# Prologue of a fused attention and MLP block: later first-norm stores, later w2, four tiles transposed on TensorE

## The chip, the cores and the metric

The kernel runs on one core of a Trainium2 chip. The metric is the time on the device in microseconds (us): the median of five runs. A profile of one further execution shows where the time goes.

## The reference

The input x has 2048 rows (tokens) of 1024 values. It is normalised row by row; the result `xn` goes into two branches, and their outputs are added to x. Branch B is what this case is about: it normalises `xn` again, multiplies by w1, applies gelu, shifts four groups of columns by one or two tokens, multiplies by w2, and goes on to a second MLP with w3 and w4. Branch A is an attention with a recurrent memory over segments of 32 tokens; it takes most of the kernel's time and is not touched.

```python
def _layernorm(x, axis=-1, eps=1e-05):
    m = jnp.mean(x, axis=axis, keepdims=True)
    v = jnp.var(x, axis=axis, keepdims=True)
    return (x - m) / jnp.sqrt(v + eps)

def _B_ref(x, w1, w2, w3, w4):
    h = _gelu(_layernorm(x, axis=-1) @ w1)
    ...
    hs = jnp.concatenate([g0, g1, g2, g3], axis=-1) @ w2
    x1 = x + hs
    h2 = _gelu(_layernorm(x1, axis=-1) @ w3) @ w4
    return x1 + h2

x = A_x
xn = _layernorm(x, axis=-1)
return x + _A_ref(xn, A_mem0, A_Wq, A_Wk, A_Wv, A_Wo, A_seg_len) + _B_ref(xn, B_w1, B_w2, B_w3, B_w4)
```

## The kernel before

The 2048 rows are 16 tiles of 128 rows, numbered n = 0 to 15. Work runs in stages on TensorE: phase one (x through both norms, times w1, gelu), phase two (times w2, plus the residual, third norm), phase three (w3 and w4), then the attention. The change lies in phase one and in what its DMAs leave for the start of phase two.

In phase one each tile goes through these steps. `load_x` (L228) brings its rows to the chip. `norm_stats` (L256) takes mean and variance on VectorE (DVE); a power on GpSimd (POOL, L272) makes two factors of them, one for the first norm, one for first and second norm together. So the second norm, `norm2` (L276), works from x directly: on DVE for n below 8 (L281), on ScalarE (ACT) from 8 on (L283). The first norm, `norm1` (L288), makes `xn`, which is kept on the chip as a residual for phase two (`xn_keep`) and stored to memory for the attention (`xn_scratch`, L292).

TensorE needs the second norm's result transposed. For tiles below `NPE` (6) TensorE does that itself: `transposes` (L299), eight matmuls with an identity per tile (L305), copied out by ACT (L306). The other tiles are transposed by a DMA that SyncE (SP) issues (L285) into the tile `xn2T`. `stage1` (L321) then multiplies by w1: for each of eight blocks of output columns, `co`, eight matmuls and one gelu on ACT (L328). It handles one tile (width 128) or a pair (width 256). Tiles 0 to 3 go singly, then the pairs (4,5) to (14,15). Functions handed to `stage1` in `between` are issued after a given block, which is how the preparation of later tiles is placed among ACT's gelus.

In this part every engine's order is the order of the code (a manual schedule); no planner moves work. A DMA issue on SP or ACT uses one of eight completion semaphores in turn, and so waits until the DMA eight issues earlier has landed. SP is a queue in order: what stands behind a waiting issue waits too. The ring of `x` tiles has 10 buffers (so x10 is loaded after the first norm of tile 0 is done with its buffer), that of second-norm tiles 3, and that of `xn2T` 3 pairs.

w2 (2 MB) is loaded by SP ahead of tile 7 in four DMAs (L250); the first two parts of w3 by SP from `norm1` of tiles 12 and 15 (L296), two more in phase two (L433), four at the start of phase three (L442). In phase two (L410) each tile takes 16 matmuls of width 512 (L417), two additions and statistics on DVE, a norm on ACT (L429), a DMA transpose by SP (L430), and a store of 512 KB by POOL (R1, L431); its rings have four buffers.

Of the kernel before, what the change touches and what calls it, by code (L numbers as in the profile page):

```python
# [16 lines left out]
F32 = mybir.dt.float32  # L17
# [6 lines left out]
P = 128  # L24
# [3 lines left out]
NT = S // P  # L28
# [49 lines left out]
def kernel(  # L78
# [16 lines left out]
    nc = tc.nc  # L95
    x_v = A_x[0].rearrange("(n p) d -> p n d", p=P)
# [6 lines left out]
    w2_v = B_w2.rearrange("(k p) n -> p k n", p=P)  # L103
    w3_v = B_w3.rearrange("(k p) n -> p k n", p=P)
# [7 lines left out]
    xn_v = xn_d.rearrange("(n p) d -> p n d", p=P)  # L112
# [78 lines left out]
    with tc.manual_schedule(engines={mybir.EngineType.PE, mybir.EngineType.SP, mybir.EngineType.Pool}), ExitStack() as actx:  # L191
# [6 lines left out]
        with ExitStack() as bctx:  # L198
            w3ctx = bctx.enter_context(ExitStack())
            w3_pool = w3ctx.enter_context(tc.tile_pool(name="w3", bufs=1, side="right"))  # L200
            w3_sb = w3_pool.tile([P, KT, F], BF16)

            w3_at = [0]

            def load_w3():

                c, k0 = divmod(w3_at[0], 4)
                w3_at[0] += 1
                cs = slice(c * (F // 2), (c + 1) * (F // 2))
                nc.sync.dma_start(w3_sb[:, 2 * k0:2 * k0 + 2, cs], w3_v[:, 2 * k0:2 * k0 + 2, cs])  # L210

            with ExitStack() as hctx:
                psum0 = hctx.enter_context(tc.tile_pool(name="psum0", bufs=4, space=PSUM))
# [2 lines left out]
                w2_sb = keep.tile([P, KT, D], BF16)  # L216
                xn_keep = [wpool.tile([P, 4, D], BF16, tag="w", name=f"xnk{i}") for i in range(3)] + [keep.tile([P, 4, D], BF16, name="xnk3")]

                hctx.enter_context(tc.manual_schedule(engines={mybir.EngineType.DVE, mybir.EngineType.Activation}))
                with ExitStack() as p0:  # L220
                    big = p0.enter_context(tc.tile_pool(name="p0big", bufs=1))
                    ring = p0.enter_context(tc.tile_pool(name="p0ring", bufs=3))
                    w1_sb = big.tile([P, KT, D], BF16)
                    NPE = 6

                    xts = {}

                    def load_x(n):  # L228
                        if n < NT:
                            xts[n] = ring.tile([P, D], BF16, tag="xt", bufs=10, name=f"xt{n}")  # L230
                            if n == 0:
                                nc.scalar.dma_start(xts[n][:, 512:], x_v[:, n, 512:])
                                nc.sync.dma_start(xts[n][:, :512], x_v[:, n, :512])
                            else:
                                (nc.gpsimd if n == 12 else nc.sync).dma_start(xts[n][:], x_v[:, n, :])

                    m0 = hTB[:M, 0, 16:16 + D]
                    nc.gpsimd.dma_start(m0, A_mem0[0])
# [7 lines left out]
                        q.dma_start(w1_sb[:, 2 * c:2 * c + 2, :], w1_v[:, 2 * c:2 * c + 2, :])  # L246
                    for n in range(3, 7):
                        load_x(n)
                    for i in range(4):
                        nc.sync.dma_start(w2_sb[:, 2 * i:2 * i + 2, :], w2_v[:, 2 * i:2 * i + 2, :])  # L250
                    for n in range(7, 10):
                        load_x(n)

                    stats = {}

                    def norm_stats(n, part=None):  # L256

                        if n >= NT:
                            return
                        xt = xts[n]  # L260
                        if n not in stats:
                            stats[n] = [ring.tile(shape, F32, tag=tag, bufs=6, name=f"{tag}{n}") for tag, shape in (("st", [P, 2, 6]), ("mv", [P, 2]), ("ab", [P, 2]), ("rr", [P, 2]), ("nm2", [P, 1]))]
                        st, mv, ab, rr, nm2 = stats[n]
                        if part in (None, 0):
                            nc.vector.bn_stats(st[:, 0, :], xt[:, 0:512])
                        if part == 0:
                            return
                        nc.vector.bn_stats(st[:, 1, :], xt[:, 512:1024])
                        nc.vector.bn_aggr(mv[:], st[:])
                        nc.vector.scalar_tensor_tensor(ab[:], epsm[:], mv[:, 1:2], epsa[:], op0=ALU.mult, op1=ALU.add)  # L270
                        for c in (slice(1, 2), slice(0, 1)) if n == 0 else (slice(0, 2),):
                            nc.gpsimd.tensor_tensor(rr[:, c], ab[:, c], neghalf[:, c], op=ALU.pow)  # L272
                        if n >= 8:
                            nc.gpsimd.tensor_scalar(nm2[:], mv[:, 0:1], rr[:, 1:2], -1.0, op0=ALU.mult, op1=ALU.mult)
# [13 lines left out]
                    def norm1(n):  # L288
                        st, mv, ab, rr, nm2 = stats[n]
                        xn = xn_keep[n // 4][:, n % 4]  # L290
                        nc.vector.tensor_scalar(xn, xts[n][:], mv[:, 0:1], rr[:, 0:1], op0=ALU.subtract, op1=ALU.mult)
                        nc.gpsimd.dma_start(xn_v[:, n, :], xn)  # L292
                        if n < 3:
                            load_x(n + 10)
                        if n in (12, 15):
                            load_w3()  # L296
                        return xn

                    def transposes(xn2, xn2T, jj, half, halves=False):  # L299
# [21 lines left out]
                    def stage1(n0, nt, xn2T, between, j0=0):  # L321
                        w = nt * P
                        for co in range(KT):
                            ps = psum.tile([P, 512], F32, tag="mm", bufs=4)
                            for k in range(KT):
                                nc.tensor.matmul(ps[:, :w].rearrange("p (n t) -> p n t", t=P), w1_sb[:, k, co * P:(co + 1) * P],  # L326
                                                 xn2T[:, j0:j0 + nt, k, :], start=(k == 0), stop=(k == KT - 1))
                            nc.scalar.activation(hTB[:, co, 2 + n0 * P:2 + n0 * P + w], ps[:, :w], ACTF.Gelu_apprx_tanh)  # L328
                            for f in between.get(co, ()):
                                f()  # L330
# [13 lines left out]
                    tiles2, xn2s = {}, {}  # L344
# [6 lines left out]
                    def tr(n, half, halves=False):  # L351
                        transposes(xn2s[n], tiles2[n - n % 2], n % 2, half, halves)
# [12 lines left out]
                    nc.gpsimd.memset(hTB[:, :, S + 2:S + 4], 0.0)  # L365
                    load_consts(4)
                    nc.gpsimd.memset(sums[:], 1.0)
                    for n in range(1, 6):
                        if n > 1:
                            norm_stats(n + 1, 0)  # L370
                        norm2_of(n)
                        norm_stats(n + 1, 1 if n > 1 else None)
                        if n > 1:
                            norm1(n - 2)
                        if n == 1:
                            stage1_k(tiles2[0])
                        elif n < 4:
                            stage1(n - 1, 1, tiles2[(n - 1) // 2 * 2], {6 - n: [lambda n=n: tr(n, 0)], 7 - n: [lambda n=n: tr(n, 1)]}, (n - 1) % 2)

                    def ahead(n):  # L380
                        norm_stats(n + 1, 0)
                        norm2_of(n)
                        norm_stats(n + 1, 1)
                        if n == 6:
                            norm1(n - 2)

                    stage1(3, 1, tiles2[2], {0: [lambda: tr(4, 0)], 2: [lambda: tr(4, 1), lambda: ahead(6)], 4: [lambda: tr(5, 0)], 5: [lambda: tr(5, 1), lambda: ahead(7)]}, 1)
                    for n in range(13, NT):
                        load_x(n)

                    def prep(n):
                        norm2_of(n)
                        norm_stats(n + 1)
                        if n == 8:
                            norm1(n - 3)
                        norm1(n - 2)

                    for n0 in range(4, NT, 2):
                        between = {c: [] for c in range(KT)}
                        if n0 + 4 < NT:  # L400
                            between[1 + 2 * (n0 == 4)] += [lambda n0=n0: prep(n0 + 4)]
                            between[4 + 2 * (n0 == 4)] += [lambda n0=n0: prep(n0 + 5)]
                        stage1(n0, 2, tiles2[n0], between)
                    for n in (NT - 2, NT - 1):
                        norm1(n)

                xn3T = [wpool.tile([P, 4, KT, P], BF16, tag="w", name=f"xn3T{tb}") for tb in range(4)]
                with ExitStack() as p2:
                    ring = p2.enter_context(tc.tile_pool(name="p2ring", bufs=4))
                    for n in range(NT):  # L410
                        x1 = ring.tile([P, D], F32, tag="x1")
                        st = ring.tile([P, 2, 6], F32, tag="st")
# [7 lines left out]
                        mv = ring.tile([P, 2], F32, tag="mv")  # L420
# [14 lines left out]
            with ExitStack() as p3:  # L435
# [2 lines left out]
                big = p3.enter_context(tc.tile_pool(name="p3big", bufs=1))  # L438
                ring = p3.enter_context(tc.tile_pool(name="p3ring", bufs=2))
                w4_sb = big.tile([P, FT, D], BF16)  # L440
                for _ in range(4):
                    load_w3()  # L442
                vbT = big.tile([P, H, NSEG], BF16)
                xb = big.tile([P, KT, NSEG], BF16)
                gps = []
# [95 lines left out]
                for tb in range(4):  # L541
# [18 lines left out]
                    for j in range(4):  # L560
                        n = tb * 4 + j
# [214 lines left out]
        ahead = stage_loads([nextB[0]], 0, first_w)  # L776
        for gi_, group in enumerate(groups):
# [3 lines left out]
            for hg in range(8):  # L781
# [8 lines left out]
                if hg < 7:  # L790
                    ahead = stage_loads(Bs, hg + 1, second_w if (gi_, hg) == (0, 0) else ())
                if hg == 7 and gi_ + 1 < len(groups):
                    ahead = stage_loads([nextB[b] for b in groups[gi_ + 1]], 0)
# [236 lines left out]
```

## Time and profile before

| what | us |
|---|---|
| median of five runs (1508.13 to 1509.68) | 1509.32 |
| the profiled execution, its own time | 1508.66 |
| its span, first to last instruction | 1506.5 |
| TensorE (PE) busy in it | 1497.7 |
| phase one ends, the first matmul of phase two starts | 67.03 |
| the first matmul of phase three (w3) starts | about 122.3 |
| first weights of w1 landed, so that stage 1 can start | 8.72 |

All times inside the profile count from the start of the span. A timeline line gives start, duration, engine, line and operation, what is written and read, and how many such instructions were merged; in brackets the engine's idle time before it and what ended it. `SPq`, `ACTq` and `POOLq` are queues that issue DMAs. A line of the chain of waits gives start, duration and what the end of the program hung on in that stretch. Ends of matmuls are modelled, so a busy TensorE may be a little less busy than shown. The share of the DMA engines is above 1 in some short windows, because the packets' recorded times overlap.

DMA traffic by stretch, from the same profile (mean share of the 16 DMA engines, GB/s): 10 to 20 us 1.06 and 378; 20 to 30 us 1.11 and 279; 40 to 50 us 1.17 and 255; 60 to 70 us 0.13 and 51; 100 to 120 us 1.05 and 291.

### The profile page before, as it was taken

Reading aid. Unit: us, or ns where it says so; the run is one execution under the profiler, and the core shown is the slowest. Engines: PE = TensorE matmul, PEld = TensorE weight load, DVE = VectorE, ACT = ScalarE, POOL = GpSimd, SP = SyncE. Lnnn points to the kernel's source line nnn. Section 1 sums busy time; section 2 is a strip of 40 time slices with the busy share of each in tenths; the row PEclk is TensorE's granted clock in tenths of the full one; section 3 lists DMA queues with packets and bytes.
Section 4 is the critical chain, followed back from the end, with each engine's and each line's share of the span. In section 5 each row is a group of like instructions: output and inputs, shape, how many; then the busy total and the mean of one; then the engine's idle time right before and its main releaser. Section 6 shows DMA issues by size and latency. Waiting matters only on the chain.

```text
span 1506.5 us, 24248 instructions
## 1 busy us (share of the span) xinstructions
PE 1497.7 (99%) x9757; PEld 803.5 (53%) x9828; DVE 546.8 (36%) x1148; ACT 502.3 (33%) x1140; POOL 175.9 (12%) x250
## 2 busy tenths in 40 slices
PE   9999999999999999999999999999999999999999
PEld 8744444445454444444466645664665455545555
DVE  8382230100010112211246624651564166516643
ACT  5533103013012011111156614650663166406630
POOL 6231020211211221100000000001000100010001
PEclk9999999999999999999999999999999999999999
DMA  9699752353455777622399957992997299918911
GB/s 306 158 271 322 218 173 93 134 203 113 154 157 143 187 239 252 215 98 84 126 222 248 245 132 175 252 244 69 240 252 203 71 230 223 216 63 207 209 49 51
DMA packets 305426, 272.89 MB, mean 181 GB/s; under 512 B 156022, under 2 KB 272536, under 8 KB 305312
## 3 DMA queue, kind: packets, MB, share of 16 engines
q1 hardware_dynamic: 282656, 188.98, 50.5%
q0 software_dynamic: 21824, 81.08, 15.5%
q8 instruction: 79, 1.29, 0.4%
q10 hardware_dynamic: 832, 1.25, 0.2%
q14 instruction: 35, 0.29, 0.1%
HBM read 190.05 MB, written 45.29 MB: 156 GB/s over the span
## 4 chain that ended last, share of the span: by engine, by line
PE 98%; DMA 1%; issue 0%; ACT 0%; SPq 0%; DVE 0%; ACTq 0%
PE ps L669 30%; PE ps L603 15%; PE pso L727 15%; PE ps L546 13%; PE ps L572 13%; PE ps L417 4%; PE ps L326 3%; PE psO L708 2%; PE psS L684 2%; DMA xn2T<-xn 1%; PE ps L867 1%; PE ps L498 1%; PE gps L481 0%; PE ps L467 0%; DMA w_sb<-in_B_w_dram 0%
## 5 line engine op out<-in xcount | busy, mean ns | idle before, releaser
L669 PE MATMUL ps<-hTb,wt 128*128 128x396 bf16 (+2 forms) x2528 | 484.8, 342 | 0.0
L669 PEld LDWEIGHTS <-wt 128*128 128x128 bf16 x2528 | 236.7, 98 | 175.6 <-DMA wt<-in_A_Wq_dram 0.2
L603 PE MATMUL ps<-wt,xT 128*128 128x512 bf16 x1004 | 220.1, 379 | 1.1
L727 PE MATMUL pso<-wo_sb,oX 128*128 128x512 bf16 (+1 forms) x972 | 208.3, 372 | 1.1
L546 PE MATMUL ps<-xn3T,w_sb 128*128 128x512 bf16 x896 | 196.2, 379 | 0.0
L572 PE MATMUL ps<-w_sb,h3T 128*128 128x512 bf16 x873 | 194.1, 379 | 1.2
L603 PEld LDWEIGHTS <-xT 128*128 128x128 bf16 x1024 | 100.2, 98 | 120.8
L547 ACT ACTIVATE h3T<-ps 128x512 bf16<-128x512 f32 x112 | 66.9, 597 | 290.7 <-PE ps L546 289.8
L727 PEld LDWEIGHTS <-oX 128*128 128x128 bf16 x992 | 96.4, 98 | 107.6
L671 ACT CAST KT<-ps 128x462 bf16<-128x462 f32 (+2 forms) x160 | 81.8, 512 | 202.7 <-PE ps L669 198.5
L572 PEld LDWEIGHTS <-h3T 128*128 128x128 bf16 x896 | 87.0, 98 | 103.6
L546 PEld LDWEIGHTS <-w_sb 128*128 128x128 bf16 x896 | 86.7, 98 | 102.2
L690 DVE TENSOR_REDUCE sums<-sm 99x4 f32<-99x396 f32 (+2 forms) x176 | 97.6, 555 | 114.8 <-ACT sm L688 114.8
L673 ACT ACTIVATE QT<-ps 128x462 bf16<-128x462 f32 (+2 forms) x160 | 84.0, 525 | 120.4 <-PE ps L669 106.2
L605 ACT CAST Vs<-ps 128x512 bf16<-128x512 f32 x64 | 37.5, 586 | 232.1 <-PE ps L603 223.5
L686 DVE TENSOR_TENSOR sm<-psS,c_mask_reg_sb 99x396 f32<-99x396 f32 x152 | 86.7, 571 | 72.4 <-PE psS L684 72.2
L609 DVE CAST Vs<-ps 128x512 bf16<-128x512 f32 x64 | 44.3, 692 | 171.6 <-PE ps L603 166.0
L688 ACT ACTIVATE sm<-sm 99x396 f32<-99x396 f32 (+2 forms) x176 | 93.0, 528 | 34.7 <-DVE sm L686 28.1
L696 DVE TENSOR_TENSOR Pn<-sm,rs 99x396 bf16<-99x396 f32 (+2 forms) x176 | 98.9, 562 | 6.5 <-DMA PT<-Pn 0.6
L734 POOL DMA_DIRECT2D out_dram<-ot x30 | 16.4, 548 | 698.5 <-DVE ot L733 698.5
L573 DVE TENSOR_TENSOR R<-ps,R 128x512 f32<-128x512 f32 x32 | 22.0, 690 | 182.6 <-PE ps L572 172.5
L733 DVE TENSOR_TENSOR ot<-pso,Rt 128x512 bf16<-128x512 f32 (+1 forms) x33 | 22.3, 675 | 166.5 <-PE pso L727 162.3
(131 smaller groups left out, 1049.8 us busy)
## 6 DMA issues: line engine op xcount, KB each, us to landing
wt<-in_A_Wq_dram SPq DMA_DIRECT2D x76, 512.0 KB
wt<-in_A_Wk_dram SPq DMA_DIRECT2D x76, 512.0 KB
wt<-in_A_Wv_dram POOLq DMA_DIRECT2D x24, 1024.0 KB, 6.5
V_scratch<-Vs SPq DMA_DIRECT2D x32, 512.0 KB
V<-V_scratch SPq DMA_DIRECT2D x40, 384.0 KB
R_scratch<-x POOLq DMA_DIRECT2D x16, 512.0 KB, 4.1
R<-R_scratch SPq DMA_DIRECT2D x16, 512.0 KB
R_scratch<-R POOLq DMA_DIRECT2D x16, 512.0 KB, 3.4
```

Source lines behind the costliest of these rows:

```text
L546: nc.tensor.matmul(ps[:].rearrange("p (n t) -> p n t", t=P), w3_sb[:, k, f * P:(f + 1) * P], xn3T[tb][:, :, k, :], start=(k == 0), stop=(k ...
L547: nc.scalar.activation(h3T[:, f, :], ps[:], ACTF.Gelu_apprx_tanh)
L572: nc.tensor.matmul(ps[:], h3T[:, f, j * P:(j + 1) * P], w4_sb[:, f, ch * 512:(ch + 1) * 512], start=(f == 0), stop=(f == FT - 1))
L603: nc.tensor.matmul(ps[:], xT[:, m4 * 4 + j, k, :], wv[:, k, :], start=(k == 0), stop=(k == KT - 1))
L669: nc.tensor.matmul(ps[:, :nb], w[:, k, hh * P:(hh + 1) * P], B["hT"][:, k, :nb], start=(k == 0), stop=(k == KT - 1))
L671: nc.scalar.copy(dst[:, hh, :], ps[:, :nb])
L673: nc.scalar.mul(dst[:, hh, :], ps[:, :nb], scale)
L686: nc.vector.tensor_tensor(sm[:T, :, :T], S3, t["mask"][:].unsqueeze(1).to_broadcast((T, 4, T)), op=ALU.add)
L688: nc.scalar.activation(e[:T, :, :T], sm[:T, :, :T], ACTF.Exp, scale=LN2)
L690: nc.vector.tensor_reduce(ss, e[:T, :, :T], axis=AX.X, op=ALU.add)
L696: nc.vector.tensor_tensor(Pn[:T, :, :T], e[:T, :, :T], rs[:T, :].unsqueeze(2).to_broadcast((T, 4, T)), op=ALU.mult)
L727: nc.tensor.matmul(self.ps[:, :self.w], self.oX[0][:, h, self.oX[1] + self.gl * P:self.oX[1] + (self.gl + 1) * P], wo_sb[:, h, self.cc], s ...
```

## The change

- `NPE` goes from 6 to 4: tiles 4 and 5 are transposed by DMA, as those after them.
- Tiles 4 and 5 go through `stage1` singly, no longer as a pair.
- `norm1` no longer stores its tile and loads no w3. It stands later: for tiles 0 and 1 after the second norms of tiles 4 and 5, for the others two at a time from the preparation of tile 9 on. `load_x(n + 10)` hangs on it for every tile; x10, x11 and x12 are loaded by POOL, the rest by SP.
- The first-norm rows are stored at the end of phase one by SP, in four DMAs of four tiles each.
- w2 is loaded in two halves, after the pairs (6,7) and (12,13); the first two parts of w3 follow the stores, and the last four parts are loaded in two DMAs of double size.
- Preparation of tile n0+3 comes after block 0 of the pair (n0, n0+1), that of n0+4 after block 4; before, those of n0+4 and n0+5 came after blocks 1 and 4. Small statistics tiles get other numbers of buffers.

```diff
-            def load_w3():
+            def load_w3(w=1):
                 c, k0 = divmod(w3_at[0], 4)
-                w3_at[0] += 1
+                w3_at[0] += w
...
-                nc.sync.dma_start(w3_sb[:, 2 * k0:2 * k0 + 2, cs], w3_v[:, 2 * k0:2 * k0 + 2, cs])
+                nc.sync.dma_start(w3_sb[:, 2 * k0:2 * (k0 + w), cs], w3_v[:, 2 * k0:2 * (k0 + w), cs])
...
-                    NPE = 6
+                    NPE = 4
...
-                                (nc.gpsimd if n == 12 else nc.sync).dma_start(xts[n][:], x_v[:, n, :])
+                                (nc.gpsimd if n in (10, 11, 12) else nc.sync).dma_start(xts[n][:], x_v[:, n, :])
...
-                    for i in range(4):
-                        nc.sync.dma_start(w2_sb[:, 2 * i:2 * i + 2, :], w2_v[:, 2 * i:2 * i + 2, :])
                     for n in range(7, 10):
                         load_x(n)
+
+                    def load_w2(i):
+                        nc.sync.dma_start(w2_sb[:, 4 * i:4 * i + 4, :], w2_v[:, 4 * i:4 * i + 4, :])
...
                         nc.vector.tensor_scalar(xn, xts[n][:], mv[:, 0:1], rr[:, 0:1], op0=ALU.subtract, op1=ALU.mult)
-                        nc.gpsimd.dma_start(xn_v[:, n, :], xn)
-                        if n < 3:
-                            load_x(n + 10)
-                        if n in (12, 15):
-                            load_w3()
+                        load_x(n + 10)
...
-                    for n in range(1, 6):
+                    for n in range(1, 4):
...
-                        if n > 1:
-                            norm1(n - 2)
                         if n == 1:
                             stage1_k(tiles2[0])
-                        elif n < 4:
+                        else:
                             stage1(n - 1, 1, tiles2[(n - 1) // 2 * 2], {6 - n: [lambda n=n: tr(n, 0)], 7 - n: [lambda n=n: tr(n, 1)]}, (n - 1) % 2)
-
-                    def ahead(n):
+                    for n in range(4, 8):
                         norm_stats(n + 1, 0)
                         norm2_of(n)
                         norm_stats(n + 1, 1)
-                        if n == 6:
-                            norm1(n - 2)
-
-                    stage1(3, 1, tiles2[2], {0: [lambda: tr(4, 0)], 2: [lambda: tr(4, 1), lambda: ahead(6)], 4: [lambda: tr(5, 0)], 5: [lambda: tr(5, 1), lambda: ahead(7)]}, 1)
-                    for n in range(13, NT):
-                        load_x(n)
+                        if n < 6:
+                            norm1(n - 4)
+                    stage1(3, 1, tiles2[2], {}, 1)
+                    firsts = list(range(2, NT))

                     def prep(n):
                         norm2_of(n)
                         norm_stats(n + 1)
-                        if n == 8:
-                            norm1(n - 3)
-                        norm1(n - 2)
-
-                    for n0 in range(4, NT, 2):
+                        for _ in range(min(2, n - firsts[0]) if n > 8 else 0):
+                            norm1(firsts.pop(0))
+
+                    stage1(4, 1, tiles2[4], {}, 0)
+                    stage1(5, 1, tiles2[4], {4: [lambda: prep(8)]}, 1)
+                    for n0 in range(6, NT, 2):
                         between = {c: [] for c in range(KT)}
-                        if n0 + 4 < NT:
-                            between[1 + 2 * (n0 == 4)] += [lambda n0=n0: prep(n0 + 4)]
-                            between[4 + 2 * (n0 == 4)] += [lambda n0=n0: prep(n0 + 5)]
+                        for n, c in ((n0 + 3, 0), (n0 + 4, 4)):
+                            if n < NT:
+                                between[c] += [lambda n=n: prep(n)]
                         stage1(n0, 2, tiles2[n0], between)
-                    for n in (NT - 2, NT - 1):
-                        norm1(n)
+                        if n0 in (6, 12):
+                            load_w2(n0 // 12)
+                    while firsts:
+                        norm1(firsts.pop(0))
+                    for i in range(4):
+                        nc.sync.dma_start(xn_v[:, 4 * i:4 * i + 4, :], xn_keep[i][:])
+                    for i in range(2):
+                        load_w3()
...
-                for _ in range(4):
-                    load_w3()
+                for _ in range(2):
+                    load_w3(2)
```

More of the change, by code (lines that the diff above doesn't have):

```diff
@@ L261, in norm_stats @@
                         if n not in stats:
-                            stats[n] = [ring.tile(shape, F32, tag=tag, bufs=6, name=f"{tag}{n}") for tag, shape in (("st", [P, 2, 6]), ("mv", [P, 2]), ("ab", [P, 2]), ("rr", [P, 2]), ("nm2", [P, 1]))]
+                            stats[n] = [ring.tile(shape, F32, tag=tag, bufs=10 if tag in ("mv", "rr") else 4, name=f"{tag}{n}") for tag, shape in (("st", [P, 2, 6]), ("mv", [P, 2]), ("ab", [P, 2]), ("rr", [P, 2]), ("nm2", [P, 1]))]
                         st, mv, ab, rr, nm2 = stats[n]
```

## The prediction

> **What bounds the kernel now.** I read the page's busy shares first, then TensorE's timeline over the first 72 us (all that the change touches), then the chain of waits there, then the queue of SyncE, which issues the DMA transposes.
>
> ```profile
> PE 1497.7 (99%) x9757; PEld 803.5 (53%) x9828; DVE 546.8 (36%) x1148; ACT 502.3 (33%) x1140; POOL 175.9 (12%) x250
> ```
>
> TensorE has no idle time to win: 1506.5 - 1497.7 = 8.8 us in the whole span. So the change can give only TensorE work that disappears, or a gap that closes, and it can cost a gap that opens.
>
> ```profile
> 20.39 0.39 PE L305 MATMUL ps<-ident,xn 128*128 128x128 bf16 x4
> ...
> 21.50 0.39 PE L305 MATMUL ps<-ident,xn 128*128 128x128 bf16 x4
> ...
> 22.62 0.39 PE L305 MATMUL ps<-ident,xn 128*128 128x128 bf16 x4
> ...
> 23.29 0.39 PE L305 MATMUL ps<-ident,xn 128*128 128x128 bf16 x4
> 23.52 8.04 PE L326 MATMUL ps<-xn2T,w_sb 128*128 128x128 bf16 x80
> 31.78 7.15 PE L326 MATMUL ps<-xn2T,w_sb 128*128 128x256 bf16 x64 [0.22 <-ACT hTB L328]
> 39.09 28.11 PE L326 MATMUL ps<-xn2T,w_sb 128*128 128x256 bf16 x256 [0.16 <-ACT hTB L328]
> 67.03 5.34 PE L417 MATMUL ps<-w_sb,hTB 128*128 128x512 bf16 x23
> ```
>
> Four groups at L305 are the TensorE transposes of tiles 4 and 5; after the pair (4,5) there are two short gaps, 0.22 and 0.16 us; from 39.09 on the pairs (8,9) to (14,15) run without one, about 7.0 us each (28.11 / 4), and phase two begins at 67.03.
>
> ```profile
> 24.36 5.75 DMA xn2T<-xn
> ...
> 31.48 5.60 DMA xn2T<-xn
> ```
>
> These, from the chain of waits in the same 72 us, are two DMA transposes (tiles 6 and 8) with the time from issue to landing: 5.6 to 5.8 us, with x loads, w2 and first-norm stores in flight. A transpose with little beside it is faster; from the timelines of SyncE and VectorE at 190 us:
>
> ```profile
> 190.40 1.23 SPq L450 DMA_TRANSPOSE xr<-xn_scratch  x1
> ```
>
> ```profile
> 193.68 1.22 DVE L452 TENSOR_REDUCE xb<-xr 128x32 bf16<-128x1024 bf16 x1 [0.81 <-DMA xr<-xn_scratch]
> ```
>
> The reader waited for it until 193.68: 3.3 us from issue. And one directly behind a large load is slower; SyncE's timeline, then its waits:
>
> ```profile
> 50.84 0.57 SPq L210 DMA_DIRECT2D w_sb<-in_B_w_dram  x1
> 52.17 1.23 SPq L285 DMA_TRANSPOSE xn2T<-xn  x1
> 53.45 0.58 SPq L210 DMA_DIRECT2D w_sb<-in_B_w_dram  x1
> ```
>
> ```profile
> SPq L430 <- DMA xn2T<-xn: 5.5, 1, 5.5
> ```
>
> Tile 15's transpose was issued at 52.17, behind 896 KB of w3; SyncE, free at 54.03, waited 5.5 us more for it, to 59.5: 7.3 us from issue. Nobody needed it before 60 us. These three latencies, 3.3, 5.7 and 7.3, decide this case.
>
> [...] The trace shows the slow state only at the start (12 warm-up matmuls in 5.30 us, 442 ns each, where 128x512 later takes 10.74 / 49 = 219 ns)[...].
>
> **The change, part by part.** The order of the changed program and what each instruction waits for are read from its instructions; times from the rows above.
>
> Tiles 4 and 5 off TensorE: 2 x 8 matmuls of 128x128 go. The chain gives 0.22 us to four, so 4 x 0.22 = 0.89 us less. Their four ACT evictions (0.59 us each, L306) go too, beside TensorE: nothing.
>
> Tiles 4 and 5 single: 128 matmuls of width 128, at 0.0558 us (0.446 per output block of eight), for 64 of width 256 at 0.109 us (0.873 per block): 7.14 against 6.98, +0.16 us.
>
> Gaps: the ACT norm of tile 8 stood waiting for tile 6's transpose until 30.11 and held the gelus back; it now waits for an old TensorE tile. Both gaps, 0.38 us, can go.
>
> First norms late: norm1 of tiles 0 and 1 (0.54 us each on VectorE) moves behind the second norms of tiles 4 and 5; the others follow from tile 9 on. It shortens VectorE's chain less than it seems, as norm2 then waits for POOL's power (0.7 to 0.9 us, L272). The chain per tile is norm2 0.46, half statistics 0.72, aggregation and scaling 0.4, then POOL's answer about 0.9 later, 2.5 us; with a norm1 behind the scaling 2.7. From norm2 of tile 2 at 12.93 (its row before, unmoved) I get norm2 of tiles 4, 5, 6, 7 at 17.9, 20.6, 23.3, 25.8, against 18.3, 21.0, 23.75, 26.5 in VectorE's rows. Norm2 of 6 and 7 gain a wait for the transposes of 4 and 5 (buffer reuse); their statistics and stores queue behind it on VectorE. With the first-norm stores and w2 out of the way, the load of the first 4.5 MB at the 380 GB/s of these windows ends near 14 us, so these transposes run nearly alone: 3.3 us, or 4.4, which is what tile 7 took before beside three x loads and a store (27.03 to 31.45 in the record of semaphores).
> - Tile 4: issued 18.5, landed 21.8 to 22.9; TensorE wants it at 24.41 - 0.89 = 23.5. No gap.
> - Tile 5: 21.2 to 24.5-25.6, wanted at 27.1. Tile 7: 26.4 to 29.7-30.8, wanted at 23.5 + 7.14 = 30.66. At most 0.1.
>
> Second norms of tiles 9, 11, 13, 15 now come after the first output block of the pair just before theirs. From there to the need are 7.0 - 0.87 = 6.1 us; gelu (0.4) and norm (1.24) take 1.6 of it: each of these transposes has about 4.5 us. Before, they were issued a pair earlier. Alone (3.3) or in light traffic (4.4) they make it: tile 9 (block 0 of the pair (6,7) ends at 31.5, so issued 33.2 and landed by 37.6, wanted at 37.65), 13 and 15.
>
> Tile 11 doesn't. SyncE's order is: transpose 10, x14, x15, the first half of w2 (1 MB), transpose 11. Block 4 of the pair (6,7) ends at 30.66 + 5 x 0.873 = 35.0, norm2 of 10 with gelu at 36.7; so transpose 10 at 36.75, x14 38.05, x15 38.5, w2 39.0; block 0 of the pair (8,9) ends at 38.5, norm2 of 11 at 40.25, and transpose 11 is issued at 40.3 behind 1.5 MB. Wanted: 30.66 + 2 x 7.0 = 44.65. Lower end: the 1.5 MB stream from 40 to 44, the transpose's own 2 us follow: 46.0, a gap of 1.3. Upper end: as tile 15 before, 7.3 us from issue, and 0.5 us for the extra bytes: 48.1, a gap of 3.4. I take the middle, 2.4 us. The pairs after it start as much later, with slack as before.
>
> w2's second half follows transpose 15, issued near 58, landed by 63; phase two reads it at 67 to 68: hidden, by 4 us. The first-norm stores (4 x 1 MB) and two w3 loads (1.8 MB) follow on SyncE: DMA work that ran at 15 to 62 us now runs until about 78. The windows from 62 to 74 us show the DMA idle, so most fits; phase two's first transpose (75 us before) lands two or three us later, its buffers are four deep at 3.45 us a tile, and w3 is read at 122. Nothing, or below 1 us if an R1 store is held up. POOL loses 16 stores (0.6 to 0.7 us each, off the path) and gains loads of x10, x11; that helps nobody on the path. The w3 loads merged at L440 keep their place behind the last transpose of phase two; they are read from 146 us. From 122 us on the order is the same.
>
> Sum: -0.89 - 0.38 + 0.16 + 2.4 = +1.3 us against the profiled execution (1508.66 us, span 1506.5). The median of the five runs is 1509.32, 0.66 above; the difference carries over: **1510.6 us**.
>
> **Rivals.**
> 1. Tile 11's transpose is in time (TensorE's own saving stays): -0.89 - 0.38 + 0.16 = -1.1, 1508.2 us. For it: 1.5 MB at 380 GB/s is only 4 us. Against it: tile 15's 7.3 us.
> 2. Slower: transposes are never as quick as 3.3 us beside other work. From 4.5 us on, every pair waits. At 5.6 us: tile 4 +0.5, tile 7 +1.7, tiles 9, 13, 15 +1.1 each, tile 11 +2.5: 8.0 - 1.1 = +6.9, 1516.2 us. For it: tiles 6 and 8. Against it: the stores and loads that ran beside those are gone.
> 3. Slower as well: tile 11's gap reaches about 3.4 us and TensorE falls to half clock for as long: 3.5 + 1.7 - 1.1 = +4.1, 1513.4 us. For it: the upper end above. [...]
> 4. The late stores hold up phase two: R1 stores land over 13 us after issue and TensorE waits; +1 to +3 us, 1511 to 1513. Against: idle DMA at 62 to 74 us.
>
> **How the numbers follow.** Forecast 0.52, rival 1 0.20, rival 2 0.10, rival 3 0.10, rival 4 0.08. Under 0.2% (3.0 us) a measurement of this kernel can't be told from no change. The forecast and rival 1 lie within, 4 about half: same 0.75. Slower: rivals 2 and 3 and a part of 4, 0.21. Faster by 3 us would need more than all the idle time that this part has: 0.04. The range goes from rival 1 to rival 3: 1508.1 to 1513.4.
>
> **What would show it.** Right: transposes L305 (now L302) 4 tiles; no gap ahead of tile 4; one gap of 1.3 to 3.4 us ahead of the pair (10,11), released by a DMA transpose; phase two at 68 to 69 us. Wrong: gaps ahead of every pair (rival 2), N = 256 blocks of over 1 us after a gap (rival 3), a gap in phase two (rival 4), phase two at 66 us (rival 1).

## The result and the profile after

| | before, beside it | changed |
|---|---|---|
| median, us | 1509.30 | 1512.76 |
| lowest to highest, us | 1508.13 to 1510.51 | 1508.74 to 1524.36 |
| profiled execution, its own time / its span, us | 1508.66 / 1506.5 | 1512.94 / 1511.2 |
| first matmul of phase two, us | 67.03 | 71.59 |

The ratio is 1.0025 (95% interval 1.0018 to 1.0032): slower by 0.25%. The forecast was 1510.6; the value lies inside the range, 2.2 us above the forecast. The span grew by 4.7 us, and 4.56 of them are there when phase two starts. So the loss is made in phase one. The busy shares of the changed kernel, from its profile:

```profile
PE 1497.5 (99%) x9805; PEld 804.0 (53%) x9876; DVE 546.7 (36%) x1148; ACT 502.4 (33%) x1144; POOL 167.5 (11%) x236
```

TensorE's busy time is what it was (1497.5 against 1497.7), although work was taken away and the warm-up matmuls took 4.27 us for 5.30: a first hint that some of the rest ran slower. Its timeline over phase one:

```profile
18.63 26.35 PE L323 MATMUL ps<-xn2T,w_sb 128*128 128x128 bf16 x344
49.00 22.75 PE L323 MATMUL ps<-xn2T,w_sb 128*128 128x256 bf16 x192 [4.02 <-DMA xn2T<-xn]
71.59 3.62 PE L416 MATMUL ps<-w_sb,hTB 128*128 128x512 bf16 x15
```

From 18.63 to 44.98 there is not one gap: no transposes on TensorE, none of the two short stalls of before. Then it waits 4.02 us ahead of the pair (10,11). And the last three pairs take 22.75 us, where 3 x 7.03 = 21.1 were due. The windows behind the gap say why (columns: stretch and its length, then busy time and count of PE, PEld, DVE, ACT, POOL, then the granted clock, DMA share, GB/s):

```profile
49.00:50.00 1.00, 1.00 (x5) 0.73 (x6) 0.00 (x0) 0.00 (x0) 0.00 (x0) 0.50 0.31 66
50.00:51.00 1.00, 1.00 (x7) 0.71 (x5) 0.00 (x0) 0.08 (x1) 0.00 (x0) 0.50 0.00 0
51.00:52.00 1.00, 1.00 (x7) 0.69 (x6) 0.00 (x0) 1.00 (x2) 0.00 (x0) 0.50 0.00 0
52.00:53.00 1.00, 1.00 (x9) 0.83 (x8) 0.00 (x0) 0.82 (x2) 0.00 (x0) 0.83 0.00 0
53.00:54.00 1.00, 1.00 (x11) 0.90 (x10) 0.00 (x0) 0.39 (x1) 0.00 (x0) 1.00 0.42 82
```

In the record of the clock it is 0.50 from 48.94 to 52.35 us and 1.00 after; in a 1-us window at half clock 5 to 7 matmuls run instead of 11. That costs 22.75 - 21.1 = 1.7 us. The account: -0.89 - 0.38 + 0.16 (the terms of the prediction) + 4.02 (gap) + 1.7 (half clock) = +4.6, measured +4.56.

What TensorE waited for, in SyncE's timeline and in the chain of waits of the changed kernel:

```profile
36.95 1.24 SPq L286 DMA_TRANSPOSE xn2T<-xn  x1
38.24 1.10 SPq L235 DMA_DIRECT2D xt<-in_A_x_dram  x2
39.38 0.43 SPq L253 DMA_DIRECT2D w_sb<-in_B_w_dram  x1
40.44 7.26 SPq L286 DMA_TRANSPOSE xn2T<-xn  x2
```

```profile
40.44 8.51 DMA xn2T<-xn
```

Tile 11's transpose was issued at 40.44, behind x14, x15 and 1 MB of w2, and landed at 48.95, 8.5 us later. TensorE wanted it at 44.98.

### The profile page after: what moved, and what is told of

The parts are those of the page before. It is cut to its first block, busy times and chain, and to the rows that moved or that the text cites. A ratio compares the mean times of both kernels' runs of the same rounds, so it can differ in the third digit from the quotient of the medians.

```text
span 1511.2 us, 24328 instructions
## 1 busy us (share of the span) xinstructions
PE 1497.5 (99%) x9805; PEld 804.0 (53%) x9876; DVE 546.7 (36%) x1148; ACT 502.4 (33%) x1144; POOL 167.5 (11%) x236
## 4 chain that ended last, share of the span: by engine, by line
PE 98%; DMA 2%; issue 0%; SPq 0%; DVE 0%
PE ps L668 30%; PE ps L602 15%; PE pso L726 15%; PE ps L545 13%; PE ps L571 13%; PE ps L416 4%; PE ps L323 3%; PE psO L707 2%; PE psS L683 2%; DMA xn2T<-xn 1%; PE ps L866 1%; PE ps L497 1%; DMA PT<-Pn 1%; PE gps L480 0%; PE ps L466 0%; DMA w_sb<-in_B_w_dram 0%
```

## The experiments

Two questions were open: does the 1 MB of w2 in front make the gap, and what decides the half clock? A third came up on the way: why do single runs of the changed kernel reach 1524 us? Diffs are against the changed kernel, unless the text says otherwise; all ratios are against the kernel before, which ran beside each.

| kernel | 95% interval of the ratio | median, us | lowest to highest, us |
|---|---|---|---|
| first half of w2 behind transpose 11 | 0.9979 to 0.9993 | 1507.19 | 1506.6 to 1510.7 |
| 512 KB of w2 ahead | 1.0025 to 1.0055 | 1514.19 | 1508.4 to 1527.2 |
| twelve matmuls in the gap | 1.0000 to 1.0016 | 1510.66 | 1509.8 to 1514.9 |
| w2 from POOL | 1.0009 to 1.0026 | 1512.78 | 1509.5 to 1514.8 |
| w2's halves behind transposes 11 and 13 | 0.9979 to 0.9992 | 1507.24 | 1506.7 to 1508.6 |
| 512 KB ahead, early stores | 1.0036 to 1.0062 | 1517.68 | 1515.1 to 1518.5 |
| 512 KB behind transpose 11, longer tail | 1.0008 to 1.0050 | 1510.76 | 1507.2 to 1524.0 |
| w2 where it was before | 0.9986 to 1.0002 | 1508.05 | 1507.5 to 1512.0 |
| all of w2 ahead | 1.0023 to 1.0052 | 1515.38 | 1514.8 to 1516.2 |
| changed kernel again | 1.0003 to 1.0024 | 1510.27 | 1508.9 to 1519.8 |
| changed kernel a third time | 1.0017 to 1.0035 | 1513.31 | 1510.1 to 1521.8 |

**The first half of w2 behind transpose 11.**

```diff
+                            if n == 11:
+                                between[c] += [lambda: load_w2(0)]
...
-                        if n0 in (6, 12):
-                            load_w2(n0 // 12)
+                        if n0 == 12:
+                            load_w2(1)
```

> The first half of w2 goes to SyncE right behind tile 11's transpose instead of right ahead of it. Theory (the 1 MB in front of the transpose makes the gap, and the gap halves TensorE's clock): transpose 11, issued near 40.4 us, lands within 3.3 to 4.6 us, by 45; the gap ahead of pair (10,11) is 0.4 us or less; no output block of that pair takes over 1 us; phase two starts at 66 to 66.5 us, the span is 1505.3 to 1506, about 1 us under the kernel before. Transpose 12 now stands behind that 1 MB and may be late by up to 0.8 us. Rival (odd tiles are prepared too late, w2 matters little): a gap of 2 us or more stays, phase two at 68.5 us or later, not faster than before.

TensorE's timeline and SyncE's:

```profile
18.69 47.16 PE L323 MATMUL ps<-xn2T,w_sb 128*128 128x128 bf16 x536
65.69 9.66 PE L418 MATMUL ps<-w_sb,hTB 128*128 128x512 bf16 x43
```

```profile
40.35 1.24 SPq L286 DMA_TRANSPOSE xn2T<-xn  x1
41.63 0.58 SPq L253 DMA_DIRECT2D w_sb<-in_B_w_dram  x1
```

One unbroken line over the whole of phase one (the merge names the first shape; the pairs are in it). Swapping two neighbours in one queue took the gap away: transpose 11, issued at 40.35, landed at 44.11, 3.8 us later. Phase two starts at 65.69, 1.34 us before the kernel before; the prediction's terms without a gap say 1.11. All 19 executions ran at full clock. The rival falls, and this kernel is faster than both.

**All of w2 ahead, or only a quarter.** The dose, twice and half.

```diff
-                        if n0 in (6, 12):
-                            load_w2(n0 // 12)
+                        if n0 == 6:
+                            load_w2(0)
+                            load_w2(1)
```

> All of w2 (2 MB in two DMAs) stands ahead of tile 11's transpose, none behind transpose 15. Theory (what stands ahead of transpose 11 sets when it lands): after 3.1 to 3.8 us with nothing ahead, 4.2 with 512 KB, 6.0 and 8.5 with 1 MB, it now lands 9 to 12 us after its issue; gap ahead of the pair (10,11) of 4.5 to 7.5 us, half clock behind it, phase two at 71 to 75 us, median 1512.5 to 1516. Rival (stalls of the transposes' own packets make the gap, whatever stands ahead): gap of 1.5 to 4 us as with 1 MB.

From the chain of waits, then TensorE's timeline, of the kernel with 2 MB ahead:

```profile
40.39 10.46 DMA xn2T<-xn
```

```profile
50.89 22.92 PE L323 MATMUL ps<-xn2T,w_sb 128*128 128x256 bf16 x192 [5.96 <-DMA xn2T<-xn]
73.65 8.58 PE L417 MATMUL ps<-w_sb,hTB 128*128 128x512 bf16 x38
```

The transpose took 10.5 us, the gap 5.96, with the half clock behind it (22.92 for 21.1): inside all that was expected. For 512 KB, w2 was cut into four parts, one ahead of transpose 11 and three behind transpose 15:

> Only 512 KB of w2 stand ahead of tile 11's transpose, the other 1.5 MB follow transpose 15. Theory: 512 KB at 385 GB/s are 1.36 us less, so the gap falls from 4.0 to about 2.7 us, [...] and the 1.7 us of the half clock go too: phase two at about 68.6 us, 3.0 us earlier than in the changed kernel, median about 1509.7. Rival (transpose 11 is held up by stalls of its own packets, not by bytes in front): gap of 3.5 to 4 us and half clock as in the changed kernel, phase two at 71 to 71.6 us.

```profile
38.67 28.11 PE L323 MATMUL ps<-xn2T,w_sb 128*128 128x256 bf16 x256 [0.73 <-DMA xn2T<-xn]
```

Neither was right. Transpose 11 landed 4.2 us after issue, and the gap ahead of the pair (10,11) was gone, not 2.7 us (the 0.73 us in this timeline line stand ahead of the pair (8,9)): half of w2's 1 MB is worth more than 1.36 us there. The estimate took 385 GB/s; between 40 and 48 us the changed kernel's DMA moved 216 GB/s, while transposes ran among the loads. But the median rose to 1514: in the profiled execution, at 1524.58 us one of the longest of 22, TensorE stopped later, in phase three, for 10.8 us. That is the third question, taken up below.

**w2 from POOL.** The kernel with w2's first half behind transpose 11, its DMA issued by POOL: at 40.05 us, half a microsecond ahead of transpose 11 (40.56), but in another queue.

```diff
-                        nc.sync.dma_start(w2_sb[:, 4 * i:4 * i + 4, :], w2_v[:, 4 * i:4 * i + 4, :])
+                        (nc.gpsimd if i == 0 else nc.sync).dma_start(w2_sb[:, 4 * i:4 * i + 4, :], w2_v[:, 4 * i:4 * i + 4, :])
```

> The first half of w2 is issued by POOL at about 40 us, so at the same time as in the changed kernel but not in SyncE's queue. If it is the order within SyncE's queue that holds up transpose 11: it lands within 3.3 to 4.6 us of issue, gap under 0.5 us, phase two at 66 to 66.5 us. If it is the shared bandwidth of the 16 DMA engines: it lands 7 to 8.5 us after issue, as in the changed kernel, gap of 2.5 to 4 us, phase two at 70 to 71.6 us. I expect something between, nearer to the second, 6 us from issue and a gap of 1.5 us.

```profile
47.99 22.80 PE L323 MATMUL ps<-xn2T,w_sb 128*128 128x256 bf16 x192 [2.89 <-DMA xn2T<-xn]
```

Transpose 11 landed at 47.95, 7.4 us after issue; the gap was 2.89 us, and the clock halved behind it (22.80 for 21.1). So another queue didn't help here: w2's packets began at 41.6 us, those of transpose 11 at 43.6, so w2's bytes were under way first. The recorded guess, 6 us and a gap of 1.5, was too low.

**The clock.** Matmuls on zeros in the gap, and then the gap alone, measured in another place.

```diff
+                        if n0 == 10:
+                            ps = psum0.tile([P, 4, P], F32, tag="tr", name="warm2")
+                            for i in range(12):
+                                nc.tensor.matmul(ps[:].rearrange("p a b -> p (a b)"), wz[:, :P], wz[:], start=(i == 0), stop=(i == 11))
                         stage1(n0, 2, tiles2[n0], between)
```

> Twelve matmuls of 128x512 on zeros (12 x 0.22 = 2.6 us) stand on TensorE between the pairs (8,9) and (10,11); their result is read by nothing. Theory (a long idle stretch halves the clock): they fill 2.6 us of the gap, 1.4 us stay idle, all output blocks of pair (10,11) take 0.87 us, phase two at about 69.9 us instead of 71.6, median 1.7 us under the changed kernel's, about 1511. Rival (the two slow blocks come from something else that the late transpose brings): the first two blocks still take 3.4 us together and phase two starts at 71.6 us.

```profile
45.94 2.54 PE L399 MATMUL warm<-wz 128*128 128x512 bf16 x11
48.69 21.13 PE L323 MATMUL ps<-xn2T,w_sb 128*128 128x256 bf16 x192 [0.21 <-DMA xn2T<-xn]
```

That is TensorE's timeline. The transpose came late again (48.64; without the zeros TensorE would have stood idle for about 2.8 us), yet the three pairs took 21.13 us: full clock. Twelve of 13 executions had it, against 20 of 59 of the changed kernel (below), and the median is 2.1 us below the changed kernel's. (The profiled one, 1514.94 us, lost 2.2 us to a late part of w3 in phase three, and the clock behind that.)

The second kernel is the one before, with 48 idle stretches ahead of phase one, made by a chain of three VectorE instructions of eight lengths:

```diff
...
+                    for e in range(48):
+                        w = (512, 1024, 1536, 2048, 2560, 3072, 3584, 4096)[e * 5 % 8]
+                        nc.vector.tensor_copy(gx[:, 0:1], ps[:, 0:1])
+                        nc.vector.tensor_tensor(gx[:, :w], gx[:, :w], gx[:, :w], op=ALU.add)
+                        nc.vector.tensor_copy(gz[:], gx[:, :P])
+                        ps = psum.tile([P, 512], F32, tag="mm", bufs=4, name="gap")
+                        for i in range(40):
+                            nc.tensor.matmul(ps[:], gz[:], wz[:], start=(i == 0), stop=(i == 39))
```

> The kernel before with 48 idle stretches of TensorE put in at the start, of eight lengths, each made by a chain of three DVE copies and additions (0.9 us for the shortest, 2.6 to 4.8 us for the longest, as DVE turns out) and followed by 40 matmuls of 128x512 (8.6 us). It measures from which idle time the granted clock halves. View A [...]: every stretch under 3.4 us leaves the clock at 1.00. View B [...]: stretches over 3 us always halve it, those of 2 to 3 us in part of the cases, those under 1.7 us never; each time the next 3.4 us run at half clock and cost 1.7 us.

```profile
29.10 8.81 PE L354 MATMUL gap<-wz,gz 128*128 128x512 bf16 x39 [1.48 <-DVE gz L351]
40.72 10.49 PE L354 MATMUL gap<-wz,gz 128*128 128x512 bf16 x39 [2.81 <-DVE gz L351]
53.22 8.81 PE L354 MATMUL gap<-wz,gz 128*128 128x512 bf16 x39 [2.01 <-DVE gz L351]
63.24 8.81 PE L354 MATMUL gap<-wz,gz 128*128 128x512 bf16 x39 [1.21 <-DVE gz L351]
74.59 10.49 PE L354 MATMUL gap<-wz,gz 128*128 128x512 bf16 x40 [2.55 <-DVE gz L351]
```

In this timeline the number in brackets is the idle time, and the second column shows what it did: 40 matmuls take 8.81 us, or 10.49 when a half clock follows. Over the 47 stretches between such groups:

| idle stretch, us | 0.94 to 1.75 | 2.01 | 2.28 | 2.55 | 2.81 |
|---|---|---|---|---|---|
| followed by half clock | 0 of 23 | 2 of 6 | 0 of 6 | 4 of 6 | 6 of 6 |

Each half clock of this profile lasts 3.413 us in the record of the clock, and all begin on one grid of that period. The changed kernel's record agrees: its clock changes at 48.94, 52.35 and 1513.25 us, 1 and 428 times 3.413 us apart. Call one period of the grid a window. Of the 47 stretches, the 35 that left at most 1.96 us of idle time in any one window were not followed by a half clock, and the 12 that left 2.01 us or more in one were. View A, which is what the prediction's rival 3 assumed, falls. View B's ranges hold as far as they were tried: 12 of the 24 stretches of 2.01 to 2.81 us were followed by a half clock, none of the 23 up to 1.75 us, and the cost was 10.49 - 8.81 = 1.68 us; none was over 2.81 us. The other profiles of this case show the same: between start-up and end, ten windows with 2.06 to 3.41 us of idle time were each followed by a half clock, and no window with 1.87 us or less was. In the changed kernel's own profile the window from 45.52 to 48.94 was idle throughout, so that profile alone could not tell the views apart; w2 from POOL, with 2.80 us in its window, could.

**The changed kernel again.**

> The changed kernel once more, unchanged, beside the kernel before on the same chip as the run with early w2. A gap of 3 to 4.5 us ahead of the pair (10,11) and, since 2.0 us of idle time within one window of 3.41 us halve the clock, 3.4 us at half clock behind it; median 1512 to 1513.5. If the gap of its profiled execution was chance, this one shows less than 2 us and a full clock.

```profile
46.91 21.13 PE L323 MATMUL ps<-xn2T,w_sb 128*128 128x256 bf16 x192 [1.52 <-DMA xn2T<-xn]
```

> The changed kernel a third time, for the spread of its gap: 1.5 to 4.2 us ahead of the pair (10,11), with a half clock behind it where at least 2.0 us of it fall into one window of 3.41 us; phase two at 67.5 to 71.6 us; median 1510 to 1513.

```profile
48.28 21.14 PE L323 MATMUL ps<-xn2T,w_sb 128*128 128x256 bf16 x192 [1.87 <-DMA xn2T<-xn]
```

The first of these expectations missed: the gap isn't constant. In the second the median, 1513.31, lies just above what was expected. These two lines, again from TensorE's timeline, show 1.52 and 1.87 us, both at full clock. Of 59 executions in the three measurements 39 have a mean clock below 1.000 (one halved window makes 0.999); their median is 1513.05 us, that of the 20 others 1510.2. The record of landings shows what varies. In the three profiles w2's first half landed at 47.92, 45.87 and 47.19, and transpose 11 at 48.95, 46.86 and 48.23: about 1.0 us later each time. In all eight profiled executions that have some of w2 ahead of it, from 512 KB to 2 MB and from either queue, it landed 0.8 to 1.0 us after the last of those bytes. So transpose 11 follows w2, and w2's 1 MB took 8.5, 6.7 and 7.4 us from its issue. What makes that time vary isn't settled. In the execution with 8.5 us, eight transpose packets between 39.4 and 46 us took over 0.8 us, up to 2.5, with a median of 0.018; in the one with 6.7 us twelve did, none over 1.02.

**The third question: the tail behind transpose 15.** In the run with 512 KB ahead, 512 KB more stood behind transpose 15, ahead of 4 MB of stores and two parts of w3. Its TensorE timeline, its waits of ACT (in all, how many, the longest), and its SyncE timeline in phase two:

```profile
143.13 17.10 PE L548 MATMUL ps<-xn3T,w_sb 128*128 128x512 bf16 x68 [10.75 <-ACT h3T L549]
```

```profile
ACT xn L431 <- DMA xn3T<-xn: 28.0, 7, 11.4
```

```profile
78.55 9.53 SPq L432 DMA_TRANSPOSE xn3T<-xn  x3
...
89.34 19.51 SPq L432 DMA_TRANSPOSE xn3T<-xn  x4
...
109.58 36.38 SPq L432 DMA_TRANSPOSE xn3T<-xn  x8
```

Four transposes of phase two are issued in 19.5 us, where TensorE makes a tile in 3.45; the last eight take 36.4 us. SyncE's timeline of the kernel with w2's first half behind transpose 11 has 12.4 and 25.5 us for the same ones:

```profile
87.45 12.40 SPq L431 DMA_TRANSPOSE xn3T<-xn  x4
...
101.27 25.47 SPq L431 DMA_TRANSPOSE xn3T<-xn  x8
```

ACT's third norms wait for them (28.0 us in seven waits: four buffers), phase three's gelus stand behind those norms on ACT, and TensorE, with its four buffers of results full, waits for the gelus. Two kernels test whether the tail does it. One has no 512 KB ahead of transpose 11, only the longer tail:

```diff
+                            if n == 11:
+                                between[c] += [lambda: load_w2(0)]
...
-                        if n0 in (6, 12):
-                            load_w2(n0 // 12)
+                        if n0 == 12:
+                            for i in range(1, 4):
+                                load_w2(i)
```

(w2 in four parts of 512 KB.)

> The first 512 KB of w2 behind transpose 11, the other 1.5 MB behind transpose 15: against the kernel with the first half behind transpose 11 only 512 KB more stand ahead of the late stores. Theory (the size of the pile behind transpose 15 decides whether phase two's transposes fall behind): no gap in phase one, phase two at 65.7 us, but waits of TensorE from 120 us on in many runs, median 1509 to 1514, spread over 5 us. Rival (the waits in phase three came of something else): 1507.2 us, spread of 2 us.

Phase two began at 65.65 without a gap, and still the runs spread from 1507.2 to 1524.0 us. The profiled execution was one of the shorter, 1509.51 us, and shows the same chain on a smaller scale; from SyncE's timeline and the waits of ACT and of TensorE:

```profile
90.59 17.31 SPq L432 DMA_TRANSPOSE xn3T<-xn  x4
```

```profile
ACT xn L431 <- DMA xn3T<-xn: 18.2, 5, 8.2
```

```profile
PE ps L548 <- ACT h3T L549: 2.3, 2, 1.5
```

So the theory holds: against the kernel with w2's first half behind transpose 11, 512 KB more of w2 have moved into the tail. They came as three DMAs there instead of one, though, and whether the bytes or the two further issues count was not tried. The other kernel takes the stores out of the tail:

```diff
+                        nc.gpsimd.dma_start(xn_v[:, n, :], xn)
                         load_x(n + 10)
...
-                    for i in range(4):
-                        nc.sync.dma_start(xn_v[:, 4 * i:4 * i + 4, :], xn_keep[i][:])
```

(on the kernel with 512 KB ahead.)

> The kernel with only 512 KB of w2 ahead of transpose 11 had no gap there, but TensorE waited 10.8 us in phase three, because phase two's transposes landed ever later. Here that kernel stores the first norms as before the change, tile by tile from POOL right after each first norm. Theory (the 4 MB of late stores, with w2 and w3 behind them, fill the DMA into phase two, and its transposes and R1 stores fall behind): without them no wait of TensorE in phase three, median 1507.5 to 1509.5, spread of about 2 us as before. The stores now run beside transposes 9 to 15, so a gap of up to 1.5 us ahead of a pair is possible. Rival (w2's 1.5 MB and w3 behind transpose 15 do it, not the stores): waits in phase three stay, median near 1514.

```profile
32.10 7.15 PE L324 MATMUL ps<-xn2T,w_sb 128*128 128x256 bf16 x64 [1.31 <-DMA xn2T<-xn]
42.21 15.80 PE L324 MATMUL ps<-xn2T,w_sb 128*128 128x256 bf16 x128 [2.96 <-DMA xn2T<-xn]
61.09 14.14 PE L324 MATMUL ps<-xn2T,w_sb 128*128 128x256 bf16 x115 [3.07 <-DMA xn2T<-xn]
```

The wait in phase three is gone, as expected, but the time isn't: its TensorE timeline shows three gaps in phase one, 7.3 us in all, where transposes 7, 9 and 13 now run beside stores (5.6, 7.4 and 7.5 us from issue). So the late stores are part of what makes the DMA transposes of this change quick enough. That the stores in the tail make the wait in phase three is less firm: with the gaps phase two also began later, and the tail had more time.

**w2 elsewhere.** Where else could it stand? Where it was before the change, or with both halves moved up:

```diff
+                    for i in range(4):
+                        nc.sync.dma_start(w2_sb[:, 2 * i:2 * i + 2, :], w2_v[:, 2 * i:2 * i + 2, :])
                     for n in range(7, 10):
                         load_x(n)
...
-                        if n0 in (6, 12):
-                            load_w2(n0 // 12)
```

> The changed kernel with w2 loaded where it was before the change: by SyncE in four DMAs ahead of tile 7's rows; everything else stays. Theory (of the change's late transfers only the stores have to be late; w2 early does no harm, since it has landed before the first DMA transpose is issued at 18.4 us, and it leaves 1 MB less in the pile behind transpose 15): transpose 11 lands within 4.5 us, no gap of over 0.5 us in phase one, full clock, no wait in phase three, median 1507 to 1508, spread of 2 us. Rival (w2 early delays tiles 7 to 9 and the first transposes, which is why it had to go): gaps of 1 us or more ahead of tile 4 or the pairs (6,7) and (8,9), phase two at 67 us or later, median over 1508.5.

```profile
19.08 47.16 PE L322 MATMUL ps<-xn2T,w_sb 128*128 128x128 bf16 x536
```

No gap, full clock in all 13, phase two at 66.08 us; the median just misses the expected span, and single runs reach 1512. So w2 didn't have to be late for the transposes. The second:

```diff
+                            if n in (11, 13):
+                                between[c] += [lambda n=n: load_w2(n // 13)]
...
-                        if n0 in (6, 12):
-                            load_w2(n0 // 12)
```

> Both halves of w2 leave the places of the change: the first goes behind transpose 11, the second behind transpose 13 (not 15). So the pile of late transfers behind transpose 15 is 1 MB smaller and starts with the first-norm stores at about 55.6 us. Theory (phase one is settled by the first half's place; the pile only adds rare slow runs): no gap in phase one, phase two at 65.7 us, median as with the first half alone moved, 1507.2 us within 0.3, and no run above 1509. Rival (the second half now holds up transpose 14 as the first held up 11): transpose 14, issued near 50.8 us and wanted at 58.6, lands after 58.6, gap ahead of the pair (14,15).

```profile
38.51 28.11 PE L323 MATMUL ps<-xn2T,w_sb 128*128 128x256 bf16 x256 [0.30 <-DMA xn2T<-xn]
```

Its profiled execution has one gap of 0.30 us, ahead of the pair (8,9), and phase two at 66.45 us, later than the expected 65.7 (stage 1 itself began 0.3 us later). Transpose 14 landed at 57.1, in time. Its median is that of the kernel with the first half alone moved, 1507.2 us, and none of its 21 executions was above 1508.57, where one of that kernel's 19 reached 1510.71. That the smaller tail does this is not shown: the kernel with w2 where it was before has as little in its tail, and three of its 13 executions were above 1509.5. Of the places tried, this one has the narrowest spread.

## Why the prediction came out as it did

- **TensorE's own terms** (-0.89, -0.38, +0.16): right. With the gap taken away phase two starts 1.34 us earlier, where the sum says 1.11; the forecast of 1508.2 for that case was 1 us too high. About half of that is time outside the span, which the prediction carried over unchanged: time less span has a median of 2.25 us before and 1.78 in the kernel with w2 behind. What lowers it stays open; with all of w2 ahead of transpose 11 it was 2.18 again.
- **Transposes of tiles 4, 5 and 7, and VectorE's chain**: right. They landed at 21.59, 24.76 and 30.71, tile 4's 0.2 us ahead of its lower bound, the others within theirs. Tile 9, said to be in time by 0.05 us, was late by 0.4 and 0.9 us in the two further profiles of the changed kernel.
- **The place of the gap**: right, and so are SyncE's times up to the issue of transpose 11 (40.3 said, 40.44 measured).
- **The size of the gap**: 2.4 us was taken out of 1.3 to 3.4. Three profiled executions of the changed kernel show 4.02, 1.52 and 1.87; the first is beyond the upper end, and the other two are small also because tile 9's lateness had already delayed TensorE. The term behind it, "the 1.5 MB stream from 40 to 44", is wrong: the DMA moved 216, 257 and 248 GB/s between 40 and 48 us, not 380, and w2 landed at 47.9, 45.9 and 47.2.
- **The step that failed is the clock.** The forecast had a gap of 2.4 us and no half clock, because rival 3 tied the half clock to a gap of about 3.4 us; that was an assumption, not shown by any profile of before. In the kernel with 48 idle stretches 2.01 us within one window of 3.413 us were enough. An estimate from these two figures: a gap of 4 us puts that much into one window wherever it falls; one of 2.4 does so in (3.41 - 2.4 + 2 x 0.4) / 3.41 = 53% of the positions; one of 1.9 never. So the half clock, 1.7 us, belonged to the forecast as an even chance, not to a rival with 0.10. The 20 executions at full clock have a median of 1510.2 us, close to the forecast of 1510.6; the other 39 make the median. That 1512.76 still lies inside the range is owed to rival 3, which set its upper end (1513.4); as to the forecast itself it is luck.
- **Rival 2** didn't happen in the profile of the changed kernel: apart from tiles 11 and 12, and tile 6 with tile 7's transpose beside it (6.0 us), transposes of phase one took 3.0 to 4.5 us, and none but tile 11's was waited for. It happened where the stores ran beside them (5.6 to 7.5 us with early stores). **Rival 4** happened in no profiled execution of the changed kernel, but 512 KB more in the tail bring it about in full, with 10.8 us of waiting where it allowed 1 to 3, through the transposes of phase two rather than through the R1 stores. (Its time, 1511 to 1513, is also half a microsecond under its own sum, 1510.6 plus 1 to 3.) That it is behind the few executions above 1516 us (5 of 59) is likely, and not shown: none of those was profiled.

## What to carry to other kernels

A load moved "later" in a queue has a new neighbour: look for the small urgent transfer that is now behind it, and swap the two; here that was worth 5.6 us between the medians (1512.76 and 1507.19). Price a gap on TensorE by its length and by the clock: in these runs 2.01 us or more of idle time in one 3.413-us window cost 1.7 us on top, so by estimate two gaps of 1.5 us, if they don't share a window, may be cheaper than one of 2.5, and matmuls on zeros paid for themselves there (median 1510.66 us for 1512.76). And a pile of transfers put behind the last urgent one isn't free when the next stage lives on DMA transposes too (with 512 KB more in it, the highest of the runs went from 1510.7 to 1524.0 us): keep it small, and look at the highest of the runs, not at the median alone.

## What the runs showed of the hardware

- In the kernel with 48 idle stretches the half clocks lasted 3.413 us each and stood on one grid of that period. Up to 1.96 us of idle time in a window left the next at full clock (35 cases), 2.01 us or more was followed by exactly one window at half clock (12 cases). Where idle time went on, two and three windows in a row were halved (all of w2 ahead, 6.8 us; 512 KB ahead, 10.2 us).
- Transpose 11 (256 KB) landed 3.1 to 3.8 us after issue behind x14 and x15 alone, 4.2 with 512 KB of w2 in front as well, 6.0 to 8.5 with 1 MB, and 10.5 with 2 MB; with some of w2 ahead it landed 0.8 to 1.0 us after the last of it. The DMA moved 216 to 257 GB/s between 40 and 48 us in three profiles of the changed kernel, while loads and transposes were mixed, and 387 to 394 when only w3 and w4 were loaded (140 to 160 us of the changed kernel).
- Packets of the transposes (256 bytes, 18 ns in the median) now and then took 0.8 to 2.5 us: in the changed kernel 38 of them between 40 and 60 us, in the kernel with w2 behind transpose 11 none there, though it has some between 20 and 40 us, where the changed kernel has 52. Where they come from was not tried.
